# Another fixed order for one kernel's operations: a layernorm, a gated GLU and an S4 convolution on one core

## The chip, the core and the metric

The kernel runs on one core of a Trainium2 chip. A core has a matrix engine (TensorE, PE), whose weight loads (PEld) overlap its matmuls, a vector engine (VectorE, DVE), an activation engine (ScalarE, ACT), GpSimd (POOL), and a sequencer that mostly issues DMAs (SyncE, SP). Each engine takes its instructions in the order in which the program lists them for it, and waits at an instruction until what that one needs is there. Sixteen DMA engines move data between HBM, the on-chip SBUF and HBM scratch. Matmul results go to PSUM. The metric is device time of the whole launch in microseconds (us).

## What is computed

`A_u` is 2048 tokens of width 512, in bf16. The reference, cut to what matters:

```python
x = A_u
xn = layernorm(x)                                  # over the 512 channels
# A: an S4 layer; 128 complex modes per channel, d = 512
logdA = exp(log_dt) * (A_re + 1j * A_im);  dB = exp(log_dt) * (B_re + 1j * B_im)
K = einsum("dn,dnl,dn->dl", C_re + 1j * C_im, exp(logdA[:, :, None] * l), dB).real   # l = 0..2047
y = causal_convolution(xn, K) + xn * Dskip         # by FFT of length 4096
# B: a gated GLU
h = sigmoid(xn @ w_gate) * (xn @ w_up)             # 512 -> 1792
out = x + y + h @ w_down                           # 1792 -> 512
```

## The kernel before

**GLU.** The tokens are worked in four groups of 512. For each group there are 14 blocks of 128 hidden channels. A *gate* (`fg`, L1036) and an *up projection* (`fu`, L1060) are four matmuls of 128x512 each, about 0.86 us on PE; a block of group 0 may have its gate in two halves. ACT takes the sigmoid of a gate (L1048, L1051). The up result is either copied by ACT to `us_sb` (L1072, the block numbers listed in `UEV`) and then multiplied by DVE, or multiplied by DVE straight from PSUM (L1076). When the 14 products of a group are there, four *down projections* (`fd`, L1105, 14 matmuls, 3.0 us each; the last one of group 3 in two halves) follow. For groups 0 to 2 ACT copies each result to SBUF, and POOL adds `x` to it with an accumulating load from HBM (`facc`, L1142).

**Input.** Layernorm statistics and scaling run on DVE and ACT (L541 to L553). Group 0 is transposed on PE. For groups 1 to 3 the normalised rows go to HBM (`x_scr`) and come back through a DMA transpose (L580) into `xnT`.

**Convolution.** It is done as a two-stage transform over the tokens.
- The *transforms* (`fx2`, L694) write to PSUM, ACT copies them out, and they go to HBM (`z_scr`), sixteen stores in all.
- The *kernel table* is made in four chunks of 128 channels: DVE builds complex powers (`cmul`, L735 to L741, and `squares`, L794), ACT squares and copies, and 64 small PE matmuls per half chunk (`f_k`, L820) make the table. It goes out to `k_scr` in eight stores. After chunks 1 and 3, half of it comes back (`kr`, L836), DVE adds `Dskip` to one row (`f_ds`, L841), and from then on it can be used. The buffers of chunk 2 are cleared by POOL (L769) once chunk 1's matmuls are done.
- The *scan units* are 16 (two channel halves of eight): load a part of `z_scr` (`zx`), two rounds of small PE matmuls (`fm`, L882, and later `fv`, L926), a product of the table with constants (`fk`, L904) in between, four half swaps (by DMA for the first half, by DVE, L895, for the second), two DVE products (L909, L913), a copy by ACT, and a store to `v_scr`.
- At the end `reload()` brings `v_scr` back, and `s2_mm` (L985, L988) makes the *outputs*, pairwise for tiles 0 to 11 (`final`) and together with the down projections of group 3 for tiles 12 to 15. `f_rt` (L955) prepares a small correction for the last tiles; `fi` (L999) puts the GLU's result into PSUM ahead of an output.

**Filler.** Operations 18 to 25 (`keep_warm`, L521) are matmuls on zeros.

**What sets the order.** The kernel is built as a list of 966 operations, each on a fixed engine, with what it depends on, and with the buffers that it takes and gives back. The list `ORDER` is a permutation of their numbers. `_Plan.run` goes through it: it hands out buffers in that sequence and yields the operations, and every engine gets its own in that sequence. So `ORDER` fixes the order of instructions on PE, DVE, ACT, POOL and of the DMAs on SP's queue, and which buffer is used for what. Nothing is reordered later. The costs and due times that stand beside the operations aren't used by this run. A DMA on SP's queue that waits for its data holds the ones behind it.

Operation numbers used below: 0 to 17 loads of inputs (9 and 12 the halves of `w_up`, 13 and 15 tiles 8 to 11 and 12 to 15 of the input, 16 `w_down`, 8 and 17 constants); 105, 107 ACT's normalisations of tiles 4 and 6; 109 and 110 the first `x_scr` store and the transpose that follows it; 141 ACT's normalisation of tile 14, 143 and 144 the last such pair; 155 the last transforms, 471 the first `fm`; 274 the last table matmuls of chunk 1, 276 to 279 the way out and back of the first table, 478 its first `fk`; 369 the last table matmuls of chunk 3; 290 POOL's clearing for chunk 2; 677, 682, 757, 762, 837, 842 the six accumulating loads; 378 a memset on POOL; 600 `f_rt`; 872 the last `fi`; 923 and 903 the up projections of blocks 9 and 5 of group 3.

Of the kernel before, what the change touches and what calls it, by code (L numbers as in the profile page):

```python
# [178 lines left out]
def _consts():  # L179
# [20 lines left out]
ON_DVE = (88, 91, 106, 108, 123, 124, 125, 139, 140, 186, 196, 197, 200, 201, 203,)  # L200
ON_ACT = (2,)
ORDER = [
# [43 lines left out]

class _Op:
    __slots__ = ("alt", "tab", "eng", "cost", "fn", "prio", "acq", "rel", "dma", "left", "users", "ready", "start", "done", "seq", "mode")
# [946 lines left out]
```

## Time and profile before

| what | value |
|---|---|
| time, three runs | 217.81, 218.6, 220.23 us; median 218.6 |
| profiled execution: span from its first to its last instruction | 217.6 us, 4946 instructions |
| mean granted TensorE clock | 1.000 |
| busy | PE 209.0, PEld 104.0, DVE 193.8, ACT 179.5, POOL 18.8 us |
| DMA | 42.80 MB, mean 197 GB/s |
| chain that ended last | PE 64%, DMA 17%, ACT 8%, SP's queue 7% |

The profiled execution is one execution; no time is given for it besides its span, which lies 1.0 us below the median of the runs and 0.2 us below the fastest. In the profile a row of the timeline has start, duration, engine, line, operation, output <- input, and what ended the idle time before it. "PE pair L985 <- DMA big<-v_scr: 0.8, 1, 0.8" in the view of waits reads: the matmuls of line 985 waited 0.8 us in total, once, 0.8 at the longest, for a DMA from `v_scr`. Most SBUF tiles lie in one tensor called `big`. A SPq row is the issue of a DMA, not its transfer; a DMA row in the chain goes from issue to landing.

### The profile page before, as it was taken

What the parts mean: (1) busy time and instruction counts of PE and PEld (TensorE: products, weight loads), DVE (VectorE), ACT (ScalarE), POOL (GpSimd) and SP (SyncE); (2) the same over time, 40 slices, a digit from 0 to 9 for tenths busy, and PEclk for the clock granted to TensorE, in tenths of its full rate; (3) what the DMA queues carried; (4) which work ended last, traced back from release to release, by engine and by line L of the source; (5) the groups of instructions that cost most, each with busy time, mean ns of one, the idle gap of its engine ahead of it and who ended that gap; (6) DMA issues with size and microseconds to landing.
All of it is one profiled execution on the core that took longest, in us unless ns stands there. A gap on an engine that the chain in (4) does not pass through costs nothing.

```text
span 217.6 us, 4946 instructions
## 1 busy us (share of the span) xinstructions
PE 209.0 (96%) x1876; PEld 104.0 (48%) x1876; DVE 193.8 (89%) x438; ACT 179.5 (83%) x286; POOL 18.8 (9%) x40
## 2 busy tenths in 40 slices
PE   7979999999999999989999999999999999999894
PEld 2435444444444454435455565445546556544463
DVE  3989999999999999999999999999999999970433
ACT  3799999999999999869989999976897999960111
POOL 1410202002100020012000002010800000000000
PEclk9999999999999999999999999999999999999999
DMA  6999936001463689865697679929959969984974
GB/s 186 316 369 390 299 116 146 0 3 48 145 156 97 233 249 156 264 143 105 166 271 202 183 224 209 239 79 216 216 116 252 282 188 263 267 245 139 269 256 166
DMA packets 51530, 42.80 MB, mean 197 GB/s; under 512 B 16434, under 2 KB 43571, under 8 KB 51507
## 3 DMA queue, kind: packets, MB, share of 16 engines
q1 hardware_dynamic: 50338, 40.60, 63.8%
q0 software_dynamic: 864, 1.57, 5.5%
q10 hardware_dynamic: 304, 0.33, 0.6%
q8 instruction: 14, 0.23, 0.4%
q14 instruction: 10, 0.07, 0.1%
HBM read 25.97 MB, written 12.85 MB: 178 GB/s over the span
## 4 chain that ended last, share of the span: by engine, by line
PE 64%; DMA 17%; ACT 8%; SPq 7%; issue 2%; DVE 0%; ACTq 0%
PE bank L1060 18%; PE bank L1036 16%; PE bank L1105 10%; PE pair L904 7%; SPq L421 7%; DMA wu_sb<-in_B_w_up_dram 5%; PE pair L926 4%; ACT big L287 4%; DMA z_scr<-big 3%; DMA big<-big 3%; DMA big<-z_scr 2%; DMA v_scr<-big 2%; PE pair L882 2%; PE pair L820 2%; ACT us_sb L1072 2%
## 5 line engine op out<-in xcount | busy, mean ns | idle before, releaser
L287 ACT ACTIVATE big<-pair 128x1024 bf16<-128x1024 f32 x64 | 66.2, 1060 | 4.9 <-PE pair L926 1.5
L1060 PE MATMUL bank<-xnT,wu_sb 128*128 128x512 bf16 x224 | 54.5, 380 | 0.5 <-DMA wu_sb<-in_B_w_up_dram 0.4
L1036 PE MATMUL bank<-xnT,wg_sb 128*128 128x512 bf16 (+1 forms) x220 | 50.7, 368 | 1.9 <-DMA wg_sb<-in_B_w_gate_dram 1.8
L1105 PE MATMUL bank<-wd_sb,hT_sb 128*128 128x512 bf16 (+1 forms) x238 | 50.4, 367 | 0.0
L1036 PEld LDWEIGHTS <-wg_sb 128*128 128x128 bf16 x236 | 22.2, 98 | 26.9 <-issue 2.5
L1105 PEld LDWEIGHTS <-hT_sb 128*128 128x128 bf16 x238 | 22.6, 98 | 25.2 <-issue 1.9
L1060 PEld LDWEIGHTS <-wu_sb 128*128 128x128 bf16 x224 | 20.6, 98 | 25.2 <-issue 3.0
L1048 ACT ACTIVATE hT_sb<-bank 128x512 bf16<-128x512 f32 x52 | 30.9, 636 | 1.2 <-PE bank L1036 1.1
L735 DVE TENSOR_TENSOR big<-big 128x1024 bf16<-128x1024 bf16 (+4 forms) x40 | 26.8, 670 | 0.3 <-ACT big L287 0.2
L736 DVE TENSOR_TENSOR big<-big 128x1024 bf16<-128x1024 bf16 (+4 forms) x40 | 26.7, 667 | 0.0
L1072 ACT ACTIVATE us_sb<-bank 128x512 bf16<-128x512 f32 x40 | 25.9, 648 | 0.3
L909 DVE TENSOR_TENSOR big<-big 128x2048 bf16<-128x2048 bf16 x16 | 19.5, 1218 | 0.6 <-PE pair L926 0.3
L904 PE MATMUL pair<-big 128*128 128x256 bf16 x160 | 19.8, 273 | 0.0
L789 ACT ACTIVATE sq_sb<-big 128x256 bf16<-128x256 bf16 (+2 forms) x20 | 13.8, 691 | 5.1 <-DVE big L741 4.9
L904 PEld LDWEIGHTS <-big 128*128 128x128 bf16 x160 | 15.4, 98 | 4.9 <-issue 1.0
L1076 DVE TENSOR_TENSOR hT_sb<-hT_sb,us_sb 128x512 bf16<-128x512 bf16 x40 | 16.5, 418 | 0.4 <-ACT us_sb L1072 0.3
L740 DVE TENSOR_TENSOR big<-big 128x512 bf16<-128x512 bf16 (+4 forms) x40 | 16.5, 414 | 0.1
L741 DVE TENSOR_TENSOR big<-big 128x512 bf16<-128x512 bf16 (+4 forms) x40 | 16.5, 413 | 0.0
L1007 ACT ACTIVATE big<-pair 128x1024 bf16<-128x1024 f32 x3 | 3.1, 1023 | 15.2 <-PE pair L985 12.4
L895 DVE COPY big<-big 32x1024 bf16<-32x1024 bf16 x32 | 13.4, 419 | 0.6
L1011 DVE TENSOR_TENSOR big<-pair,glu_sb 128x1024 bf16<-128x1024 f32 x2 | 2.5, 1226 | 11.7 <-PE pair L985 8.1
L541 DVE BATCH_NORM_STATS2 stats<-big 128x6 f32<-128x512 bf16 x15 | 9.8, 682 | 3.4 <-DMA big<-in_A_u_dram 3.4
(104 smaller groups left out, 244.3 us busy)
## 6 DMA issues: line engine op xcount, KB each, us to landing
big<-c_E SPq DMA_DIRECT2D x16, 320.0 KB, 3.9
z_scr<-big SPq DMA_DIRECT2D x16, 256.0 KB, 2.9
big<-z_scr SPq DMA_DIRECT2D x16, 256.0 KB, 4.9
v_scr<-big SPq DMA_DIRECT2D x16, 256.0 KB, 3.1
big<-in_A_u_dram SPq DMA_DIRECT2D x4, 512.0 KB, 8.2
big<-big SPq DMA_DIRECT2D x32, 64.0 KB, 3.6
wu_sb<-in_B_w_up_dram SPq DMA_DIRECT2D x2, 896.0 KB, 10.7
wd_sb<-in_B_w_down_dram SPq DMA_DIRECT2D x1, 1792.0 KB, 15.1
```

The source lines that it names most:

```text
L287: nc.scalar.activation(out=get(out), in_=get(in_), func=ACT.Identity)
L735: V.tensor_tensor(out=wide(outp), in0=wide(lo), in1=mre, op=ALU.mult)
L736: V.tensor_tensor(out=wide(tb()), in0=wide(lo), in1=mim, op=ALU.mult)
L740: V.tensor_tensor(out=outp[:, :, 0], in0=outp[:, :, 0], in1=tb()[:, :, 1], op=opr)
L741: V.tensor_tensor(out=outp[:, :, 1], in0=outp[:, :, 1], in1=tb()[:, :, 0], op=opi)
L904: T.matmul(two(sk)[:, o:o + DW], es()[:, g, kt, :], kTv[p][:, :, kt, :], start=kt in (0, NKT - 1), stop=kt >= NKT - 2)
L909: V.tensor_tensor(out=pp().rearrange("p q h m -> p (q h) m"), in0=xx().rearrange("p q h m -> p (q h) m"), in1=kb()[:, 0:2 * DW].unsqueeze( ...
L1036: T.matmul(bank(sl, k % 2)[:, c0:c1], w[:, kt, k * 128:(k + 1) * 128], xnT[:, grp, kt, c0:c1], start=(kt == 0), stop=(kt == KT - 1))
L1048: S.activation(out=hT_sb[:, hs.idx, k % 2, :], in_=bank(sl), func=ACT.Sigmoid)
L1060: T.matmul(bank(sl), wu_sb[:, kt, k * 128:(k + 1) * 128], xnT[:, grp, kt, :], start=(kt == 0), stop=(kt == KT - 1))
L1072: S.activation(out=us_sb[:, us.idx, :], in_=bank(sl), func=ACT.Identity)
L1105: T.matmul(bank(po)[:, 0:c[1] - c[0]], hT_sb[:, hts[k // 2].idx, k % 2, jj * 128:(jj + 1) * 128], wd_sb[:, k, c[0]:c[1]], start=first and ...
```

## The change

Only `ORDER` is another permutation. Operations, engines, buffers and their counts stay. Some lines of the diff with places that are spoken of below:

```diff
 ORDER = [
-    0, 1, 2, 14, 28, 38, 26, 29, 27, 3, 30, 39, 49, 32, 31, 40, 33, 41, 35, 18, 34, 4, 42, 43, 50, 24, 10, 44, 19,
-    51, 36, 45, 46, 11, 20, 52, 25, 5, 7, 37, 6, 53, 9, 47, 21, 48, 98, 96, 54, 643, 94, 663, 668, 55, 12, 644, 664,
...
-    559, 923, 847, 534, 23, 895, 924, 915, 535, 935, 850, 858, 600, 925, 601, 947, 851, 854, 950, 852, 853, 855,
-    948, 856, 859, 848, 845, 949, 951, 860, 952, 954, 865, 862, 861, 958, 857, 866, 849, 953, 867, 863, 955, 959,
-    956, 864, 962, 872, 869, 868, 963, 870, 957, 871, 960, 873, 874, 875, 961, 964, 965]
+    0, 1, 2, 14, 28, 38, 26, 29, 27, 3, 30, 39, 49, 32, 31, 40, 33, 41, 35, 18, 34, 4, 42, 43, 50, 24, 10, 44, 19, 51,
+    36, 45, 46, 11, 20, 52, 25, 5, 7, 37, 6, 22, 23, 47, 12, 54, 53, 48, 94, 96, 21, 95, 55, 98, 648, 663, 643, 664,
...
+    559, 847, 947, 842, 600, 851, 850, 950, 859, 601, 852, 855, 854, 848, 860, 853, 954, 856, 865, 948, 951, 949, 866, 862,
+    958, 861, 857, 867, 872, 959, 952, 849, 863, 953, 868, 869, 955, 864, 956, 960, 873, 962, 957, 874, 963, 961, 875,
+    870, 871, 964, 965, 375]
```

The two lists sorted by engine, at the places that matter (G1.4 g is the gate of block 4 in group 1, u its up projection, "down" a down projection; numbers are operations where they help):

```
SP, loads at the start
  before  x0 x1 x2-3 dskip par id x4-7 w_gate(2) par w_gate(1) w_gate(0) w_up(0)=9 w_up(1)=12 x8-11 x12-15 w_down=16
          109 S1=8 110 M2=17 ...
  after   x0 x1 x2-3 dskip par id x4-7 w_gate(2) par w_gate(1) w_gate(0) w_up(1)=12 x8-11 w_up(0)=9 x12-15
          109 M2=17 S1=8 w_down=16 110 ...
SP, around the first table
  before  zx(1) zx(6) swap zx(5) swap swap k_scr store, store E(6) E(5) swap k_scr load
  after   zx(6) zx(1) zx(5) zx(second half) swap swap k_scr store, store E(6) swap swap k_scr load
SP, at the end (v_scr stores of the last scan units, reloads 847 to 853)
  before  store 511, store 571, x 946, store 559, reload 847, store 535, reloads 850 851 853 848 845
  after   ... stores 571, 511, 535, 559, reloads 847 851 850 848 853     (846, 843, 844, 845, 946 earlier)
POOL
  before  ... f_pre, layernorm x3, clear c0, clear c1, 677 757 762, clear c2 = 290, clear c3, 682 837 842, 378, hold, hold
  after   ... f_pre, layernorm x3, 682, clear c0, clear c1, clear c2 = 290, 677 757 762, clear c3, hold, 837, 378, 842, hold
PE, start
  before  18 24 19 transpose 20 25 transpose 21 | gates 8 12 13 10 6 half 7 half half half half 9, G0.8 u ...
  after   18 24 19 transpose 20 25 22 23 transpose 21 | gates 9 12 8 10 4 6 half half half half half 5, G0.8 u ...
PE, first gates of group 1
  before  transforms, G0.7 u, G0.5 u, G1.12 g          after  transforms, G0.6 u, G0.3 u, G0.7 u, G1.4 g
PE, from the last transforms (155) to the first fm (471)
  before  155 down down down G2.2 g G2.11 g 471        after  155 down G2.0 g down G2.10 g down G2.4 g 471
PE, from the chunk 1 table (274) to its first use (478)
  both    twelve gates and up projections and one fm
PE, end
  before  ... fv(533) G3.9 u, 23, fi, 600, down, down, outputs(0), (12), (1), (13), down, fi, outputs(2), (15), (3), (14),
          half down, fi 872, outputs(4), (15), (5), half down
  after   ... fv(533) fv(557) G3.5 u, fi, down, 600, down, outputs(1), (0), down, fi, (12), (13), outputs(3), (2), (15), fi 872,
          half down, outputs(4), (14), (15), (5), half down
```

76 rows, old and new, of the table ORDER are left out of this document.

## The prediction

> **What bounds the kernel now.** I read the busy times first, then the waits of TensorE (PE), then the chain that ended last, and last the timeline at each place where that chain leaves PE. The page's first two parts and the waits of PE:
>
> ```profile
> span 217.6 us, 4946 instructions
> PE 209.0 (96%) x1876; PEld 104.0 (48%) x1876; DVE 193.8 (89%) x438; ACT 179.5 (83%) x286; POOL 18.8 (9%) x40
> DVE  3989999999999999999999999999999999970433
> PE bank L1036 <- DMA wg_sb<-in_B_w_gate_dram: 1.8, 1, 1.8
> PE bank L521 <- POOL rz L515: 1.4, 1, 1.4
> PE pair L985 <- DMA big<-v_scr: 0.8, 1, 0.8
> PE pair L882 <- DMA big<-z_scr: 0.7, 1, 0.7
> PE bank L1060 <- DMA wu_sb<-in_B_w_up_dram: 0.4, 1, 0.4
> PEld L820 <- ACT big L287: 0.5, 1, 0.5
> ```
>
> PE is busy for 209.0 of 217.6 us, and the listed waits of its matmuls are 5.1 us in all. Two of them (1.8 and 1.4) belong to the start, before any weights are there. So the only stalls that an order can take from PE in its dense part are three waits for transfers: 0.4 + 0.7 + 0.8 = 1.9 us. The second thing to see is VectorE (DVE): its digits are 8 or 9 from the second slice to the thirty-fourth. It has no room either: a stall that hits both engines goes straight to the end.
>
> The profile ends 217.6 us after it begins; the runs have a median of 218.6 (217.81 to 220.23). I work in differences to the span and add them to the median. About 1% (2.2 us) is what a measurement of this kernel can tell from no change.
>
> **What the change takes away.** The three places in the chain and the timeline, with the filler matmul of operation 22:
>
> ```profile
> 10.57 10.71 DMA wu_sb<-in_B_w_up_dram
> 21.32 1.04 PE bank L1060 x4
> ...
> 27.97 0.22 PE bank L521
> ...
> 92.49 5.05 DMA big<-z_scr
> ...
> 194.31 4.82 DMA v_scr<-big
> 199.21 3.05 DMA big<-v_scr
> 202.30 0.52 PE pair L985 x6
> ```
>
> *Up weights.* Before, the second half (operation 12) is issued behind the first (9) and lands at 10.57 + 10.71 = 21.28; the first up projection starts at 21.32. After, 12 goes ahead of 9, so 896 KB less stand in front of it: at 363 GB/s (row below) about 2.5 us earlier. PE reaches the first up projection after the same seven gates and five half gates in both orders, so the wait goes: **-0.5** (0.4 listed plus the start-up of the weight load). The first half is late next; its first user stands 5.6 us of PE work further on, and it lands near 22.7 (512 KB more than the second half does now). *Filler.* Operation 22 moves from the dense part into the start, where PE waits anyway: **-0.2**. Operation 23 moves too, but at 194 us it stood in the shadow of a product (below): 0.
>
> *Scan input.* From the last transform matmuls (operation 155) to the first use of z_scr (471), PE has three down projections and two gates before, the same and three gates after: 0.86 us more cover for a wait of 0.7: **-0.7**. One move could spend this: the layernorm of tile 14 (operation 141) moves behind some 7 us more ACT work, so that x_scr store comes later. SP has some 2 us of room between it and the last stores of z_scr, and I leave it at that.
>
> **What it adds.** *Down weights before the transpose.* The 1792 KB of w_down (operation 16) go behind the first x_scr store (109), just ahead of the transpose that makes group 1's input (110).
>
> ```profile
> x_scr<-big SPq DMA_DIRECT2D x3, 512.0 KB, 3.0
> 29.30 0.40 SPq L421 DMA_DIRECT2D x_scr<-big  x1
> 20.00:25.00 5.00, 4.58 (x24) 2.07 (x22) 4.96 (x13) 5.00 (x11) 1.27 (x2) 1.00 1.06 363
> 33.00:37.00 4.00, 4.00 (x26) 1.69 (x25) 4.00 (x11) 3.82 (x7) 1.31 (x2) 1.00 0.87 195
> 37.98 1.03 PE L1036 MATMUL bank<-xnT,wg_sb 128*128 128x512 bf16 x4
> ```
>
> (The window rows give the stretch, its length, busy time of PE, PEld, DVE, ACT and POOL, the clock, the share of the 16 DMA engines, and GB/s.) The store waits for two ACT normalisations. Seven ACT operations no longer stand ahead of them and one new one does, the copy behind an up projection that PE ends near 24.6 (12.5, where the first gate starts, 8.2 of gates, 3.9 more); the copy and the two take 2.2, so the store comes near 27.0, not 29.3, and lands 3.0 later, at 30.0. Behind it then stand 256 KB of m2 and 1792 KB: 2.1 MB at 363 GB/s is 5.8 us, to 35.8. The transpose took 0.87 x 4.0 less m2's 0.7, or 2.8 us, to 38.6. PE wants it at 37.98 - 0.5 - 0.2 = 37.3. That is a wait of 1.3 if the transfers go strictly one after another, 0 if the transpose passes between the others' packets, 2.0 if the store slips by 0.7. I take **+0.8**, nearer to the strict end, because a stretch of such loads leaves no gap (share 1.06 from 20 to 25 us).
>
> *POOL's accumulating loads.* Before, three of them (operations 677, 757, 762) leave from 80 us on, the third at 98.08. After, they stand in POOL's queue behind operation 290, a memset that waits for the table matmuls of chunk 1.
>
> ```profile
> q0 software_dynamic: 864, 1.57, 5.5%
> 98.08 0.87 POOL L1142 DMA_DIRECT2D glu_sb<-in_A_u_dram  x1 [3.17 <-ACT glu_sb L287]
> 102.36 0.21 POOL L769 MEMSET big<- 128x128 bf16 x1 [3.41 <-PE pair L820]
> 103.40:108.40 5.00, 5.00 (x27) 2.09 (x25) 5.00 (x14) 5.00 (x12) 0.00 (x0) 1.00 0.61 147
> 108.40:112.40 4.00, 4.00 (x21) 1.81 (x19) 4.00 (x11) 3.81 (x9) 0.00 (x0) 1.00 0.99 287
> 103.53 2.02 SPq L421 DMA_DIRECT2D k_scr<-kq_sb  x2
> 112.74 0.27 DVE L841 TENSOR_TENSOR big<-big,dskr 1x256 bf16<-1x256 bf16 x1
> 113.07 0.60 PE L904 MATMUL pair<-big 128*128 128x256 bf16 x4
> 157.00:162.00 5.00, 5.00 (x54) 2.24 (x54) 4.85 (x11) 4.70 (x8) 0.64 (x1) 1.00 0.64 156
> 165.24 0.28 DVE L841 TENSOR_TENSOR big<-big,dskr 1x256 bf16<-1x256 bf16 x1
> ```
>
> So all three leave POOL between about 103 and 106 us. In the same stretch the table goes out to k_scr and comes back (103.53 to 112.3), DVE fixes one row at 112.74, and PE starts on it at 113.07, with nothing to spare. PE's cover is the same in both orders: twelve projections and one scan matmul group between the table matmuls and operation 478. Six accumulating loads took 5.5% of 217.6 us of all engines, 2.0 us each, 6.0 for the three. The stretch has 0.39 x 5.0 = 2.0 us free, and an E load of 320 KB (0.9 us) leaves the front of this queue. If the rest is paid, PE and DVE both stand 3.1 us; if the loads find gaps, 0. Before, the third of these loads was in flight beside the row swaps at 100 us with no wait on PE, so I stay near the low end: **+0.6**.
>
> The second table has the same form, with DVE's row at 165.24 and PE right behind; there one accumulating load (842) moves behind operation 378, a memset that waits for the last table matmuls. Its 2.0 us meet a stretch with a share of 0.64 over 5 us, 1.8 free: **+0.2** (0 to 0.8, the share of the store and the load that it could double).
>
> *Middle.* From 78 to 88 us, gates of group 2 are drawn between the down projections and the transforms, and each takes a PSUM bank that ACT has just emptied. The page lists no such wait of PE before; the nearest row is a weight load that waited 0.5 for ACT (L820, above). Bounds 0 and 1.0 (two such waits); I take **+0.2**.
>
> *End.* The stretch that decides:
>
> ```profile
> 191.61 0.60 ACT L1072 ACTIVATE us_sb<-bank 128x512 bf16<-128x512 f32 x1
> 192.32 0.84 PE L926 MATMUL pair<-big 64*64 64x512 bf16 x16
> 192.74 0.42 DVE L1076 TENSOR_TENSOR hT_sb<-hT_sb,us_sb 128x512 bf16<-128x512 bf16 x1
> 193.26 1.02 ACT L287 ACTIVATE big<-pair 128x1024 bf16<-128x1024 f32 x1 [1.05 <-PE pair L926]
> 194.17 0.69 DVE L1076 TENSOR_TENSOR hT_sb<-hT_sb,bank 128x512 bf16<-128x512 bf16 x1 [0.41 <-PE bank L1060]
> 195.03 6.22 PE L1105 MATMUL bank<-wd_sb,hT_sb 128*128 128x512 bf16 x28
> ```
>
> Count from the end of the last scan matmuls (193.1, where the last up projection starts). Before, its product is read straight from PSUM and the down projections start at +1.9; two take 6.1, and at +8.1 PE stands before the output matmuls until +9.2. After, two scan matmul groups come back to back, so ACT copies two results (1.02 each), then the last up result (unit 47, which goes through us_sb, 0.60), then DVE multiplies (0.42): the down projections start at +2.4. Operation 600 (0.3) now stands between them, so PE is at the outputs at +8.8. The last v_scr store is issued at about +1.4, ahead of the reloads and no longer behind one, lands near +4.4, and its reload (3.05) near +7.6: no wait. That trades the wait of 0.8 for 0.5 + 0.3. Then operation 872 needs a PSUM pair that ACT frees 1.02 us after the outputs of tile pair 3, with only 0.85 us of PE work between: 0.3. Sum of the end: **+0.3** (-0.8 to +0.8).
>
> **Sum.** -0.5 - 0.2 - 0.7 + 0.8 + 0.6 + 0.2 + 0.2 + 0.3 = +0.7: a span of 218.3, a time of 218.6 + 0.7 = **219.3 us**. All else is the same work in another sequence; DVE's sum doesn't change, and the distances from DVE's results to PE's use grow a little on average.
>
> **Rivals.** *A, the gains without the new waits.* All transfers pass beside each other, ACT keeps up, and the end loses its wait without a price: -1.4 - 0.8 = -2.2, or 216.4. For it: the three old waits lose their cause, and the shares of 0.61 and 0.64 leave gaps. Against: it needs five places to come out well at once.
>
> *B, slower: POOL's and SP's transfers take turns.* The place is the first table's way out and back, the price 3.1 us there and 0.8 at the second, on PE and DVE together. With the transpose wait at 1.3 and the rest as above, the sum is +0.7 + 2.5 + 0.6 + 0.5 = +4.3, or 222.9; half of it gives 221.1. It decides as soon as the load of the table lands more than about 1.5 us later, counted from its table matmuls, than before. For it: no slack at 113.07, and a share of 0.99 just before. Against: before, accumulating loads beside SP's transfers at 94 to 100 us cost PE at most the 0.7 of the scan input. [...]
>
> *C, the change misses its mark.* The transfers that land late may only move with their producers: the z stores slip with the transforms if the middle is slow, and the wait of 0.7 stays. With the up weights and the filler gained, that is +0.7 + 0.7 = +1.4, or 220.0. It lies inside the forecast's own spread.
>
> **How the numbers follow.** The forecast with C, 218.0 to 220.6: 0.50. A: 0.23, about half of it below 216.4. B: 0.27, nearly all above 220.8. So faster by over 1%: 0.12; within: 0.60; slower: 0.28. The range for 8 in 10 cuts half of A's lower part and the upper third of B: 216.4 to 222.2.
>
> **What will show it.** In the waits of PE of the changed kernel: no row for wu_sb and none for v_scr right or wrong on the first and last gains; a row for xnT or a gate of group 1 (L1036 or L1060 near 37 us) shows the transpose wait and its size; L904 near 113 and 165 us, and DVE L841 beside it, show the tables; a row of L882 near 98 us shows that the scan input wait stayed. The start of L1105 after the last L926, 1.9 us before, should be 2.4. What would make this wrong: PE stalls in places that I took as unchanged, above all ACT's queue falling behind between 60 and 90 us, or a DVE that runs out of cover in the last scans, where before it already stands within 0.5 us of ACT.

## The result and the profile after

The changed kernel takes **227.6 us** (median of four runs, 226.52 to 227.87), the kernel before on the same chip 219.41 (four runs): a ratio of **1.0378, 95% interval 1.0305 to 1.0451**. The forecast was 219.3 us, range 216.4 to 222.2. It was wrong, on the side of rival B and 4.7 us beyond its price of 222.9. The profiled execution is the fastest of the four: 226.52 us, of which 224.4 are span. Every ratio below is against the kernel before, measured beside it on the same chip; executions more than 1.5% above the fastest of their kernel count in the medians, but not in the ratios and their intervals.

The head of the page of the changed kernel (span, busy times, and the digits of DVE and ACT):

```profile
span 224.4 us, 4927 instructions
PE 208.1 (93%) x1850; PEld 104.6 (47%) x1876; DVE 194.8 (87%) x438; ACT 179.6 (80%) x286; POOL 19.7 (9%) x40
DVE  3989999599999999999978799999999999991244
ACT  4797999599999999959985798976989699881111
```

The work is the same (PE 208.1 after 209.0, DVE 194.8 after 193.8). What is new is idle time in two places: the eighth slice (39 to 45 us) and slices 21 to 23 (112 to 129 us), where DVE and ACT fall to 5 to 8. The waits of PE name them. Lines of the changed kernel are one lower than before, so L1035 is the gate and L903 the first scan matmul on the table:

```profile
PE bank L1035 <- DMA xnT<-x_scr: 3.0, 1, 3.0
PE bank L1035 <- DMA wg_sb<-in_B_w_gate_dram: 2.5, 1, 2.5
PE pair L903 <- DVE big L840: 2.1, 1, 2.1
PE bank L520 <- POOL rz L514: 1.4, 1, 1.4
PE pair L819 <- ACT big L286: 0.5, 1, 0.5
PE pair L998 <- ACT big L1006: 0.5, 1, 0.5
```

The three waits that were to go are gone: no row for wu_sb, z_scr or v_scr. Two new ones are there, the transpose (3.0) and the first table (2.1). The chain and the timeline show what stood before them:

```profile
30.51 10.12 DMA xnT<-x_scr
40.67 1.04 PE bank L1035 x4
...
107.67 4.86 DMA k_scr<-kq_sb
...
114.49 5.96 DMA big<-c_E
120.50 2.19 PE pair L903 x10
```

```profile
105.40 1.62 ACT L286 ACTIVATE kq_sb<-pair 128x768 bf16<-128x768 f32 x2 [0.20 <-PE pair L819]
106.77 2.66 POOL L1141 DMA_DIRECT2D glu_sb<-in_A_u_dram  x3 [0.25 <-issue]
107.05 1.25 SPq L420 DMA_DIRECT2D k_scr<-kq_sb  x2
112.60 0.36 SPq L420 DMA_DIRECT2D big<-k_scr  x1
118.70 0.28 DVE L840 TENSOR_TENSOR big<-big,dskr 1x256 bf16<-1x256 bf16 x1 [2.27 <-DMA big<-k_scr]
119.03 1.14 PE L903 MATMUL pair<-big 128*128 128x256 bf16 x9 [2.06 <-DVE big L840]
```

The transpose takes 10.12 us from issue to landing. At the table, POOL's three loads leave at 106.77, within 0.3 us of the table's two stores. From the end of the table's last copy (107.03) to DVE's fix at 118.70 it takes 11.7 us; before it was 103.51 to 112.74, 9.2.

A third loss stands in no list of waits. Windows of the changed kernel around both stalls (columns as in the prediction; the clock is the third number from the end):

```profile
38.00:41.00 3.00, 0.33 (x2) 0.21 (x3) 3.00 (x10) 1.27 (x3) 0.00 (x0) 1.00 0.59 133
41.00:45.00 4.00, 4.00 (x21) 1.75 (x18) 1.65 (x6) 2.99 (x5) 0.00 (x0) 1.00 0.00 0
116.50:119.00 2.50, 0.41 (x2) 0.10 (x1) 0.30 (x2) 0.73 (x2) 0.00 (x0) 1.00 1.03 247
120.80:124.10 3.30, 3.30 (x13) 1.74 (x12) 3.30 (x8) 2.96 (x5) 0.00 (x0) 0.50 0.96 289
```

Behind the table stall **TensorE's granted clock is 0.50 for 3.3 us**. PE counts as busy (3.30 of 3.30), so neither the waits nor the busy times show it, and in the page's row of clocks one digit of forty falls to 7; half of that time, 1.7 us, is lost. The first stall was followed by a clock of 1.00 in this execution.

To see where the time goes, I set the start of each PE operation against the PE work done ahead of it (every kind of operation at its unstalled spacing, from the traces), and subtract the same curve of the profiled kernel before. The result is PE's lag at equal work, in us. The kernels below the first line are the experiments of the next section:

```
                       36 us   behind      ahead of   behind     ahead of   behind    down     last
                               group 1's   the first  the first  the 2nd    the 2nd   of       outputs
                               first gate  table      table      table      table     group 3
changed kernel         -0.8     +2.5        +2.7       +7.3       +6.7       +6.7     +7.4     +6.5
e1 w_down early        -1.8     -1.5        -0.5       +5.6       +4.2       +5.4     +6.1     +5.3
e2 loads early         -0.7     +4.6        +4.9       +5.2       +4.4       +5.6     +6.4     +6.1
e3 both                -1.8     -1.5        -0.4       -0.6       -0.4       +1.0     +1.8     +1.3
e8 all three           -1.7     -1.3        -0.6       -1.2       -0.8       -0.6     -0.2     -1.1
e4 before, wd late     -0.8     +4.4        +4.1       +4.2       +4.2       +4.2     +4.2     +3.5
e5 before, loads late  -0.1     -0.1        -0.7       +5.9       +5.7       +5.7     +5.7     +5.3
x1 three gains         -0.9     -0.6        -1.0       -0.4       -0.4       -0.4     -0.4     -0.4
d1 one load late       -0.8     -0.6        -1.2       -0.8       -0.9       -0.9     -0.9     -1.1
```

Read the first line from left to right. Group 1's first gate costs 3.3, the first table 4.6, and the rest changes little. The -0.8 at the start is no gain of the change: e4 and d1, which start in the order of before, have it too. A stall of PE, once taken, was not made up in the dense part: e4 keeps its +4.2 for 160 us. One caution: the profiled execution of before is a rather long one (span 217.6; later ones have 215.5 to 218.4, most of them 216 to 217), so this scale flatters the others by about 1 us. Time outside the span was 1.9 to 2.2 us wherever a run has both numbers.

### The profile page after: what moved, and what is told of

Same layout as the page of the kernel before. It is cut to its first block, busy times and chain, and to the rows that moved or that the text cites. A ratio compares the mean times of both kernels' runs of the same rounds, so it can differ in the third digit from the quotient of the medians.

```text
span 224.4 us, 4927 instructions
## 1 busy us (share of the span) xinstructions
PE 208.1 (93%) x1850; PEld 104.6 (47%) x1876; DVE 194.8 (87%) x438; ACT 179.6 (80%) x286; POOL 19.7 (9%) x40
## 4 chain that ended last, share of the span: by engine, by line
PE 44%; DMA 18%; ACT 16%; DVE 14%; issue 3%; SPq 3%; ACTq 0%; DVEq 0%
PE bank L1104 11%; PE pair L903 8%; PE bank L1035 8%; PE bank L1059 8%; ACT big L286 5%; PE pair L925 5%; DMA xnT<-x_scr 5%; DMA big<-in_A_par_dram 4%; DMA k_scr<-kq_sb 4%; DMA big<-c_E 3%; SPq L420 3%; DVE big L734 2%; DVE big L735 2%; ACT us_sb L1071 2%; DVE big L608 2%
## 5 line engine op out<-in xcount | busy, mean ns | idle before, releaser
L286 ACT ACTIVATE big<-pair 128x1024 bf16<-128x1024 f32 x64 | 64.9, 1041 | 7.3 <-PE pair L903 3.2
L1035 PE MATMUL bank<-xnT,wg_sb 128*128 128x512 bf16 (+1 forms) x209 | 50.0, 367 | 6.3 <-DMA xnT<-x_scr 3.0
L1035 PEld LDWEIGHTS <-wg_sb 128*128 128x128 bf16 x236 | 22.1, 98 | 30.9 <-DMA xnT<-x_scr 3.4
L1059 PEld LDWEIGHTS <-wu_sb 128*128 128x128 bf16 x224 | 21.1, 98 | 25.5 <-issue 3.6
L1071 ACT ACTIVATE us_sb<-bank 128x512 bf16<-128x512 f32 x40 | 25.1, 627 | 0.4 <-PE bank L1059 0.3
L903 PE MATMUL pair<-big 128*128 128x256 bf16 x160 | 20.5, 280 | 2.6 <-DVE big L840 2.1
L903 PEld LDWEIGHTS <-big 128*128 128x128 bf16 x160 | 15.7, 100 | 8.0 <-issue 3.1
L788 ACT ACTIVATE sq_sb<-big 128x256 bf16<-128x256 bf16 (+2 forms) x20 | 13.3, 666 | 6.3 <-DVE big L740 5.4
L286 ACT ACTIVATE big<-big 128x256 bf16<-128x256 bf16 x30 | 12.4, 448 | 1.0 <-PE pair L819 1.0
L925 PE MATMUL pair<-big 64*64 64x512 bf16 (+1 forms) x256 | 13.1, 327 | 0.0
```

The costliest lines, as they stand in the source:

```text
L286: nc.scalar.activation(out=get(out), in_=get(in_), func=ACT.Identity)
L903: T.matmul(two(sk)[:, o:o + DW], es()[:, g, kt, :], kTv[p][:, :, kt, :], start=kt in (0, NKT - 1), stop=kt >= NKT - 2)
L925: T.matmul(two(sv)[o:o + 64, DW * (2 * g + y):2 * DW * (g + 1)], mab[b:b + 64, 2 * u + g, q, :], pq()[b:b + 64, q, ch] if y else pp()[b:b ...
L1035: T.matmul(bank(sl, k % 2)[:, c0:c1], w[:, kt, k * 128:(k + 1) * 128], xnT[:, grp, kt, c0:c1], start=(kt == 0), stop=(kt == KT - 1))
L1059: T.matmul(bank(sl), wu_sb[:, kt, k * 128:(k + 1) * 128], xnT[:, grp, kt, :], start=(kt == 0), stop=(kt == KT - 1))
L1071: S.activation(out=us_sb[:, us.idx, :], in_=bank(sl), func=ACT.Identity)
```

## The experiments

The kernels are permutations of the same list, so an edit is shown as the queue that it changes. Their order list takes other lines, so in all of them the gate is L1028, the row fix L833, the scan matmul on the table L896, and the DMA helper L413.

### Taking the two moves back, one at a time and together

```diff
 SP, e1 and e3
-15 109 17 8 16 110
+15 16 109 17 8 110
 POOL, e2 and e3
-682 c0 c1 290 677 757 762 336
+682 c0 c1 677 757 762 290 336
```

> The changed order with one move taken back: w_down (operation 16) stands again right behind the x_12 to x_15 load (15), ahead of the first x_scr store. Theory T (the transpose that makes group 1's input waits behind w_down in SP's queue, and PE loses 3.2 us there for good): the wait of PE for xnT goes from 3.0 us to at most 0.3, the transpose lands near 37 us instead of 40.6, and the time falls by about 3.2, to 224.3. Rival R (ACT and DVE fall behind in the new order anyway, so that what PE gains at 40 us it loses again before the first table): the wait goes, and the time stays at 226.5 to 227.6.

> The changed order with POOL's three accumulating loads (677, 757, 762) put ahead of the memset 290 again, each behind the operation that makes its data, so that they leave before the table of chunk 1 goes out. Theory T (they share the DMA engines with the table's store, load and E load; PE and DVE lose 4.3 us): the distance from the last table copy on ACT to DVE's row L840 falls from 11.7 us to about 9.2, and the time by 3 to 4.3, to 223 to 224.5. Rival R (the loads find gaps; the loss at 118 us comes from the sequence on PE, ACT and SP): distance and time stay within 1 us of the changed kernel, 226.5 to 227.6.

> The changed order with both moves taken back, w_down early and the three accumulating loads early. Theory T (two independent stalls, 3.2 and 4.3 us): the sum, 227.6 - 7.5 = 220 us, level with the kernel before (219.4) or up to 1.5 us below it, since the other moves gain 0.7 at the start and about 0.7 at the scan input. Rival R (the order as a whole costs PE, ACT and DVE their distance from one another): 224 or more.

Measured: e1 225.29 us, ratio 1.0284 (1.0213 to 1.0355); e2 225.66, ratio 1.0282 (1.0217 to 1.0347); e3 **220.27, ratio 1.0058 (1.0027 to 1.0090)**. Both moves together are the loss; the theory's sum holds for e3. But e1 and e2 gain 2.3 and 1.9 us by their medians where 3.2 and 3 to 4.3 were expected, and together 7.3: both times fell short of the theory. The windows of e1 and e2 show where the rest went:

```profile
113.50:117.50 4.00, 0.25 (x2) 0.08 (x1) 0.09 (x1) 0.51 (x2) 0.00 (x0) 1.00 0.66 148
117.50:121.00 3.50, 3.26 (x16) 2.32 (x17) 3.34 (x8) 1.79 (x3) 0.00 (x0) 0.51 0.87 257
```

```profile
37.00:41.00 4.00, 0.88 (x5) 0.20 (x2) 3.90 (x13) 2.44 (x4) 0.00 (x0) 0.99 0.93 156
41.00:44.50 3.50, 3.19 (x8) 1.16 (x9) 1.71 (x6) 0.60 (x1) 0.00 (x0) 0.53 0.00 0
```

In e1 (first fence) the transpose no longer waits, but the table stall has grown from 2.1 to 4.0 us and the clock is halved behind it. The table's way out and back takes 13.6 us there (103.80 to 117.41) instead of 11.7; why it is longer stays open. In e2 (second fence) it takes 9.4, the table stall is gone, and the half clock now follows the stall at group 1's gate. Each of them pays the price of the clock once, as the changed kernel does; of these four only e3, with neither stall, has a clock of 1.00 behind both places.

### Each move alone, in the kernel before

```diff
 SP, e4
-15 16 109 8 110
+15 109 8 16 110
 POOL, e5
-c0 c1 677 757 762 290 336
+c0 c1 290 677 757 762 336
```

> The kernel before with one move alone: w_down (16) goes behind the first x_scr store (109), just ahead of the transpose 110. There the store leaves at 29.3 us, 2.1 later than in the changed order, so the transpose would land 13.4 us behind it, near 42, against a want at 37.3. Theory T (strict order in SP's queue, and a gate whose clock halves after a PE stall of this length): a wait for xnT of 4 to 5 us, granted clock 0.5 for about 3.4 us behind it (1.7 more), together 5 to 6.5 us, 224 to 225.5. Rival R1 (the wait alone, no price of the clock): 222.5 to 223.5. Rival R2 (the transpose passes between w_down's packets when nothing else is changed): 219 to 220.

> The kernel before with one move alone: POOL's accumulating loads 677, 757 and 762 go behind the memset 290, as in the changed order. Theory T (they share the DMA engines with the first table's store and load): the distance from the last table copy on ACT to DVE's fix (9.2 us before) grows by 2 to 4, PE stalls as long at L904, and the granted clock falls to 0.5 for about 3.4 us behind it where the stall is over 2 us: 221 to 224. Rival R (the loads find gaps, since the sequence on PE, ACT and SP is that of before): within 0.7 of before, 218.7 to 219.4.

Measured: e4 **223.54 us, ratio 1.0214 (1.0139 to 1.0289)**; e5 **224.28, ratio 1.0247 (1.0170 to 1.0324)**. The sum of the two is 1.046; the changed kernel has 1.038. Of e4, the waits, the timeline of SP and a window, in this order:

```profile
PE bank L1028 <- DMA xnT<-x_scr: 3.7, 1, 3.7
```

```profile
29.99 0.96 SPq L413 DMA_DIRECT2D wd_sb<-in_B_w_down_dram  x1
32.17 6.37 SPq L572 DMA_TRANSPOSE xnT<-x_scr  x1
```

```profile
41.00:44.50 3.50, 3.44 (x10) 1.31 (x11) 2.11 (x5) 0.00 (x0) 0.00 (x0) 0.60 0.05 17
```

SP itself needs 6.37 us to issue the transpose while w_down's 1792 KB are in the same queue; where w_down went earlier or later it needs 2.17 (before), 2.20 (w1) and 2.36 (e1). The wait is 3.7, and the clock (0.60 over these 3.5 us) gives most of the rest of the 5.2 us that the lag grows by. Of e5, the timeline around the table, the DMA view of 102 to 116 us (queue: packets, MB, share; issues: count, KB each, median us to landing), and a window:

```profile
102.25 2.88 POOL L1134 DMA_DIRECT2D glu_sb<-in_A_u_dram  x3 [0.26 <-ACT kq_sb L279]
103.09 2.19 SPq L413 DMA_DIRECT2D k_scr<-kq_sb  x2
115.94 0.28 DVE L833 TENSOR_TENSOR big<-big,dskr 1x256 bf16<-1x256 bf16 x1 [3.48 <-DMA big<-k_scr]
116.27 2.29 PE L896 MATMUL pair<-big 128*128 128x256 bf16 x10 [4.02 <-DVE big L833]
```

```profile
q0 software_dynamic: 432, 0.79, 34.7%
k_scr<-kq_sb SPq DMA_DIRECT2D x2, 96.0 KB, 7.0
```

```profile
116.20:122.90 6.70, 6.63 (x29) 3.65 (x29) 5.82 (x11) 3.17 (x5) 0.00 (x0) 0.59 0.66 197
```

The three loads take 34.7% of 14 us of all DMA engines, 4.9 us. The two small stores of the table, 96 KB each, take 7.0 us (median) instead of the 3.4 that the same view of before gives, PE waits 4.0, and the clock stays down twice as long (6.8 us, to 121.7). The sequence on PE, ACT and SP is that of before, so the loads alone do it. Stores and loads were in flight together there and all of them slowed (a load took 7.2 us to land, median, where four such loads of before, in other stretches, took 4.6). Whether the two queues' transfers took turns, as rival B has it, or the engines' time as such ran out, no run here tells apart.

The other executions of these two kernels have no trace, but each has its mean granted clock. The one of e4 at 1.000 took 221.97 us, those at 0.992 took 222.96 and 224.12. The one of e5 at 0.998 took 222.69, those at 0.985 took 223.62 and 224.95. So the half clock doesn't follow in every execution, and the shortest executions are those without it.

### Moving the loads away, and only one of them near

```diff
 POOL, e6 (changed order)
-290 677 757 762 336
+290 336 677 757 762
 POOL, d1 (order before)
-677 757 762 290 336
+677 757 290 762 336
```

> The changed order with the three accumulating loads moved the other way, behind the next memset (336), which waits for table matmuls of chunk 2: they leave near 135 us, when the first table is long back. Theory T (what counts is that they meet the table's round trip, not that they are late): the distance from the last table copy to L840 is about 9.2 us, and the time 223 to 224.5, as when they leave early. Rival R1 (their data is wanted sooner than the trace shows, or the loss lies in the sequence): 226.5 or more. Rival R2 (any stretch is as full as the first table's): the stall moves to 135 us, 226 to 228.

> The kernel before with only one of the three accumulating loads (762, 256 KB) behind the memset 290; with all three there PE waited 4.0 us at the first table, and two stretches at half clock followed. Theory T (the wait goes with the bytes, the clock falls only behind a longer stall): PE waits 1.0 to 1.5 us at L904, the granted clock stays at 1.00, and the time rises by 1.0 to 1.5. Rival R (the gaps in the DMA engines, 2.0 us in this stretch, hold one load): no change, 218.6. Rival R2 (any meeting of the two queues costs the full stall): 3 us or more.

Measured: e6 226.16 us, ratio 1.0302 (1.0196 to 1.0407): a miss by its time. At the first table it does what the theory says: DVE's fix stands at 116.34, 9.3 us behind the last copy, PE has no wait there, and PE's lag against the changed kernel is 4.3 us less right behind it. Then rival R2 comes true. The loads leave at 135.74, a scan matmul waits for its input, and at the second table stands a new stall:

```profile
PE pair L896 <- DVE big L833: 2.3, 1, 2.3
PE pair L874 <- DMA big<-z_scr: 0.9, 1, 0.9
```

Together with what else moved, 2.9 of the 4.3 us are given back, and the half clock follows group 1's stall as in e2. d1: 218.95 us, ratio **1.0004 (0.9977 to 1.0030)**. One load costs nothing, against the theory that the wait goes with the bytes; it leaves POOL at 101.66, SP issues the load of the table at 106.97 (112.25 in e5), and PE waits 0.3. So the price isn't linear: one load, 1.6 us of DMA time by an estimate (a third of the 4.9 in e5), fits into that stretch, the 4.9 of three do not.

### Is it the idle PE that halves the clock?

```diff
 PE, e7 (loads early, w_down ahead of the transpose, as e2)
-G0.7 u, G1.4 g
+G0.7 u, 12 matmuls without use, G1.4 g
```

> The changed order with the accumulating loads early (225.66 us), and 12 matmuls without use (128x512, 0.2155 us each, 2.6 us; 11 of them new, one taken from the start) put on PE ahead of the first gate of group 1, into the 3.4 us in which PE waits there for the transpose. They add work and take no wait away. Theory T (the stall costs its length and, behind it, 3.4 us at granted clock 0.5, because PE was idle): the clock stays at 1.00 from 40 to 45 us, and the time falls by about 1.7, to 224. Rival R (the clock falls for another reason, or costs nothing on the path): 225.7 or a little more.

Measured: **223.64 us, ratio 1.0208 (1.0122 to 1.0293)**, 2.0 less than e2 with 2.4 us more of PE work. Its profiled execution, 224.88 us, is the longest of the four, so only the place itself is read from it:

```profile
37.19 2.75 PE L513 MATMUL bank<-glu_sb 128*128 128x512 bf16 x12
40.72 1.04 PE L1028 MATMUL bank<-xnT,wg_sb 128*128 128x512 bf16 x4 [0.78 <-DMA xnT<-x_scr]
```

```profile
37.00:41.00 4.00, 3.22 (x16) 1.31 (x15) 4.00 (x12) 1.91 (x4) 0.00 (x0) 1.00 0.48 106
41.00:44.50 3.50, 3.45 (x17) 1.61 (x17) 1.18 (x4) 2.44 (x4) 0.00 (x0) 1.00 0.00 0
```

The gate starts no earlier for it (the transpose lands when it lands), but the clock stays at 1.00 where e2 had 0.53, and all four executions have a mean of 0.998 or more where those of e2 have 0.985 to 0.992. So here it is the idle PE that halves the clock (it waits 0.8 us at this gate in e7, 3.4 in e2). For the time the evidence is weaker: the median is lower in spite of the added work, as the theory had it, but the intervals of the two ratios overlap.

### The second table, and another place for w_down

```diff
 POOL, e8 (e3 and one more)
-280 837 378 842
+280 837 842 378
 SP, w1 (e8, but w_down behind the transpose)
-15 16 109 17 8 110
+15 109 17 8 110 16
```

> The changed order with w_down early, the three accumulating loads early, and also operation 842 ahead of the memset 378 in POOL's queue, as before. Theory T (842 leaves POOL at 156.0, its 256 KB meet the second table's store, which then takes 5.1 us instead of 3.3, and PE waits 2.2 us at U1.7): the store takes about 3.3 again, the wait at the second table falls below 0.7, and the time falls from 220.3 by 1.5 to 2, to 218.3 to 218.8, level with before. Rival R (the second table is late for the sequence around it): 220 or more.

> The changed order with the accumulating loads early as before (the kernel of 219.4 us), but w_down (16) directly behind the transpose 110 in SP's queue, not early and not ahead of it. Theory T (the transpose waited only because w_down stood ahead of it in the same queue): the transpose lands near 33 us, PE waits at most 0.3 for xnT, w_down lands near 42, before the first down projection wants it, and the time is 219.4 within 0.5. Rival R (w_down's packets in flight slow the transpose whatever the order): a wait of 1 us or more at group 1's first gate, 221 or more.

Measured: e8 219.38 us, ratio 1.0054 (1.0017 to 1.0092). The wait of 1.8 us for the second table in e3 is gone, as expected, and the median is 0.9 lower where 1.5 to 2 was expected; its ratio and e3's overlap widely, so the size stays uncertain. w1: 219.45 us, ratio 1.0030 (1.0007 to 1.0052), as the theory had it. There the transpose is issued in 2.20 us instead of 7.5 and PE has no wait for it; the only wait that the move leaves, and which the theory didn't have, is a short one for w_down (SP's timeline, then PE's waits):

```profile
29.13 2.20 SPq L572 DMA_TRANSPOSE xnT<-x_scr  x1
31.38 0.57 SPq L413 DMA_DIRECT2D wd_sb<-in_B_w_down_dram  x1
```

```profile
PE bank L1097 <- DMA wd_sb<-in_B_w_down_dram: 0.5, 1, 0.5
```

So w_down may go early or directly behind the transpose, only not directly ahead of it.

### The gains alone

```diff
 x1 (order before)
-SP: 9 12           PE: 18 24 19 20 25 21        PE: 471 396 813
+SP: 12 9           PE: 18 24 19 20 25 22 23 21  PE: 471 813 396
 x2: x1, and the last 90 operations in the sequence of the changed order (but for 375, 378, 599 and 842, which stay)
```

> The kernel before with three of the moves that were forecast as gains, and none of the others: the second half of w_up (12) ahead of the first (9) in SP's queue, the fillers 22 and 23 among the first matmuls, and one gate of group 2 (813) ahead of the scan matmul 396 that waited 0.7 us for its input. Theory T (each of these gains is real, and lost in the changed order only to what happens elsewhere): wu_sb's wait of 0.4 and the scan input's of 0.7 go, and the time falls by 0.5 + 0.2 + 0.7 = 1.4, to 217.2, a ratio near 0.994. Rival R (they move waits to the next operation, whose work or bank isn't ready either): a ratio of 0.998 or more.

> The same three moves, and the last 90 operations of the changed order (two scan matmul groups at the end, the first down projection ahead of operation 600, the last v_scr store earlier), with the middle of the kernel before. At equal work PE's lag behind the kernel before fell by 0.6 to 0.9 us over this stretch in the changed kernel and in the one with all three costs undone; the forecast was +0.3. Theory T (the end is a gain of its own): 0.6 to 0.9 below the kernel with the three moves alone, 216.5, a ratio near 0.991. Rival R (the end gains only because ACT and DVE come late to it anyway): level with it, or 0.3 above.

Measured: x1 **219.0 us, ratio 1.0015 (0.9992 to 1.0039)**, x2 222.13, ratio 1.0140 (1.0106 to 1.0174). The theory falls in both. In x1 the waits for wu_sb and z_scr are gone, and nothing is gained. Its waits of PE behind the start, and the timeline at the first table:

```profile
PE pair L977 <- DMA big<-v_scr: 0.4, 1, 0.4
PE pair L556 <- DVE big L545: 0.4, 1, 0.4
PE pair L896 <- DVE big L833: 0.2, 1, 0.2
```

```profile
102.53 0.85 ACT L279 ACTIVATE kq_sb<-pair 128x768 bf16<-128x768 f32 x1
112.60 0.27 DVE L833 TENSOR_TENSOR big<-big,dskr 1x256 bf16<-1x256 bf16 x1
```

Part of the reason is in d1, which has none of these moves. Its waits of PE behind the start, down to 0.3 us, and one row of e5:

```profile
PE pair L977 <- DMA big<-v_scr: 0.6, 1, 0.6
PE pair L896 <- DVE big L833: 0.3, 1, 0.3
```

```profile
PE bank L1052 <- DMA wu_sb<-in_B_w_up_dram: 0.4, 1, 0.4
```

d1 has no row for z_scr or wu_sb either, nor has e4; the 0.4 for wu_sb is in before and in e5, where the first gate also waits longer for its weights (1.7 to 1.8 us; 1.1 in d1 and e4). So the 0.7 and the 0.4 belonged in part to the one long execution of before that was profiled, and there was less to gain than its rows say. PE's lag in x1 is -1.0 ahead of the first table and -0.4 behind it; in d1 it is -1.2 and -0.8. The table's last copy ends at 103.38 in x1 and its fix stands at 112.60, 0.1 us sooner than before (103.51, 112.74). That fits a table that hangs on ACT and DVE, so that what PE gains it waits for there, but with d1 beside it this is not shown. In x2 the end of the changed order, put behind another middle, meets a scan product that isn't ready (PE waits 1.1 us at L918 for DVE near 184 us) and waits longer for v_scr (1.2 us); it is no gain of its own.

## Why the prediction was wrong

*What was right.* The three old waits are gone from the list (-0.5, -0.7, and v_scr's 0.8 at the end), though for the first two that proves no mechanism: d1 and e4 lack them without the moves. The store of x_scr was put at 27.0 and came at 27.20; operation 600 stands between the down projections for 0.39 (0.3 forecast); the wait of operation 872 is 0.5 (0.3 forecast). Both places of added cost were named, the transpose and the first table, and so was the condition of rival B: it decides when the load of the table lands over 1.5 us later, counted from its table matmuls. By DVE's fix it was 2.5 later.

*Term "w_down ahead of the transpose", +0.8.* The mechanism was right and the size wrong, for two reasons. The 2.1 MB were put through at 363 GB/s, a row from 20 to 25 us; w_down landed at 38.24, not 35.8, the transpose at 40.63, not 38.6. (The queue here carried the transpose's small packets too: 540 of 2272 packets were under 512 B from 31 to 38 us, 1556 of 1557 from 38 to 40.6. That they were what slowed it was not tried.) Strict order was put at 1.3 us, 2.0 with a late store, and measured 3.0 to 3.7. I also chose a value below strict order although no row showed a transfer passing another in the same queue; with w_down just ahead of the transpose PE waited for it in every run, with w_down behind it not (w1). Alone the move costs 2.1%, interval 1.4 to 2.9 (e4).

*Term "POOL's accumulating loads", +0.6.* This is the step that failed. I took the low end because one load beside row swaps at 100 us had cost nothing. d1 shows that this reading was correct and proved nothing: one load is free, three together cost 4.0 us of stall. The upper bound of 3.1 was itself below the 4.0 of e5, since it priced the loads' own time and not how the table's small stores slowed beside them.

*What no term held: the clock.* Each stall that I priced was priced at its length. Most stalls of 2 to 4 us came with 3.4 us at half clock, in e5 with 6.8. Part of that can lie inside the stall (in e5 it begins at 114.88, the stall ends at 116.27), so it cost 1.4 to 1.7 us on top, in e5 2.7. With 0.8 for 3.3 at the transpose and 0.6 for 4.6 at the table, 1.7 of it the clock, the sum of +0.7 becomes 0.7 + 2.5 + 4.0 = +7.2, against 6.8 of span in the two profiles. By the medians it is 8.2; the other three executions of the changed kernel are 0.9 to 1.4 us longer than the profiled one and have no trace here. With the gains at nothing (next paragraph) and the other three added terms as forecast, the sum is 3.3 + 4.6 + 0.7 = 8.6.

*The gains, -1.4.* They came as waits that vanished, not as time. x1 has them without the costs and is level with before. I counted every wait in one profile as time that can be gained. Two of the three are not there in other kernels that have the order of before at these places (d1, e4), and the profile was a long one. That the first table, which by the same text leaves PE nothing to spare, takes back what PE gains ahead of it is possible, and not shown.

*Second table, +0.2.* The wait was 1.8 us in e3 and gone in e8, 0.9 us by their medians; in the changed kernel itself, where all comes later, PE waits 0.3 there, about as forecast. (Operation 378 waits for a DVE product and not, as the text has it, for the last table matmuls: before, it ran at 154.11, they began at 154.44. That changes little.) *Middle, +0.2:* a table matmul waits 0.5 for ACT at 83.6 us (L819), inside the bounds. *End, +0.3:* the down projections start 1.3 us behind the last scan matmuls (200.45 to 201.75), not 2.4, and PE's lag falls by 0.9 from there on, just beyond the forecast's lower bound of -0.8; x2 shows that this belongs to the whole order and is no gain that can be taken out.

*What stays open:* with all three costs undone the changed order is still 0.3 to 0.5% above before (w1, e8). Its lag grows between 51 and 94 us and again behind 165 us, in small steps for which no single wait stands; which of the many moves does it wasn't tried.

## What to carry to other kernels

A wait that appears on a full engine was paid in full here (e4's +4.2 us stood for 160 us), but a wait that vanished was worth nothing (x1, ratio 1.0015): look at more than one execution to see whether the wait is there each time, and for the next point fed by other engines, before you book a gain. Price a stall of TensorE of the lengths seen here (2.1 to 4.0 us) at its length plus a half clock that may follow (3.41 us at 0.50 in five kernels, 6.83 in e5). Where a stall can't be avoided, matmuls without use in it may pay: in e7 they held the clock at 1.00 where e2 had 0.53. When several transfers move into a stretch, add up their DMA time and the gaps there as one sum; that one of them was free says nothing of three (PE waited 0.3 us in d1, 4.0 in e5).

## What the runs showed of the hardware

A half clock of 3.41 us came with stalls of 2.1 us (changed kernel), 3.1 (e6), 3.4 (e2), 3.7 (e4) and 4.0 (e1), and one of 6.83 with the 4.0 of e5, but there was none behind the 3.0 us in the changed kernel's own first stall, nor behind 2.3 us in e6 and 1.8 in e3. So the length alone doesn't decide. Nor does PE's idle time in the last 3.41 us: up to 40.71 in the changed kernel it is 2.95, and the clock stays at 1.00, while ahead of the six drops it is 2.0 (changed kernel), 2.5 (e6), 2.6 (e5), 3.0 (e2, e4) and 3.4 (e1).

A reading with fixed steps fits the changed kernel's trace. The clock falls there at 120.68, is back at 124.09 and falls again at 223.08, behind the last matmul: these lie 1.0 and 29.0 times 3.413 us apart. Counted back from 120.68 in steps of that length, the 24th begins near 38.75. The two steps that hold most of the kernel's stalls:

```profile
38.75:42.16 3.41, 1.49 (x7) 0.69 (x8) 3.41 (x12) 0.94 (x3) 0.00 (x0) 1.00 0.26 59
117.26:120.68 3.42, 1.43 (x12) 1.14 (x13) 1.98 (x5) 0.54 (x1) 0.00 (x0) 1.00 1.09 228
```

The longer stall lies across 38.75, so PE is idle for 1.9 us of this step (and 1.0 of the one before), and the clock stays. In the other step it is idle for 2.0, and the clock falls at its end. By this reading it was luck, by the place in the step, that the longer stall cost nothing more. It is my estimate from one trace: whether the clock moves by such steps in other executions, and whether a limit lies between 1.9 and 2.0, is not shown. A stretch without any PE work wasn't needed: ahead of five of the six drops PE had worked for 0.4 to 1.4 of the 3.41 us. In e5 the clock, once down, stayed down from 114.88 to 121.71, with PE idle for 1.4 us of the first half of it.

The issue of the DMA transpose held SP for 7.5 us (30.51 to 38.04) in the changed kernel, where w_down was in the queue ahead of it, and for 2.20 in w1, where it was not. And accumulating loads beside the table's stores have no fixed price: 256 KB were free in d1 (ratio 1.0004, and PE waited 0.3 us at the table), while with 768 KB the 96 KB stores took 7.0 us, median, in e5 and 4.7 in the changed kernel, instead of the 3.4 of before.
